# Linear attention and experts on one core: rows' turn in halves in a bank of its own, loads paced by products

## The chip, the core and the metric

One NeuronCore of a Trainium2 chip runs the whole kernel. The metric is the device time of one execution in microseconds (us); the kernel before takes 340.6 us (median of three runs, 339.92 to 341.04).

## The reference

```python
f = 1.0 / (1.0 + np.exp(-f_logit))                 # q, k, v, f_logit: [4, 8, 768, 48]
for t in range(S):
    state = f[:, :, t, :, None] * state + einsum('bhd,bhe->bhde', k[:, :, t], v[:, :, t])
    y[:, :, t] = einsum('bhd,bhde->bhe', q[:, :, t], state)
x = y as rows [3072, 384]                          # one row per token
logits = x @ w_gate; e_idx = argmax(logits)        # 8 experts, one per token
gate_w = softmax(logits)[e_idx]; eom = sigmoid(x @ w_output_gate)
out[e_idx == e] = gate_w * eom[:, e] * (relu(x @ w1[e]) @ w2[e])   # w1: [8, 384, 1024]
```

## The kernel before

**Stages.** Attention handles 24 chunks of 128 tokens (4 batches of 6, `order`), all 8 heads of a chunk at once as 4 pairs. Then the eight experts run, bound by TensorE, on rows that the attention stage has scattered into DRAM (`xs_dram`) slot by slot.

**A chunk.** With p the running product of the gates and i its inverse (scans on VectorE, L218 and L225), q becomes q\*p and k becomes k\*i (GpSimd, L232 and L229; VectorE for the first and last chunk's k). `qk` (L254) makes the 128x128 products of k and q in two row halves of the array; `mask` clears their upper triangle (VectorE for one half, ScalarE and GpSimd for the other). `kn_tr` (L273) transposes k, `state` (L290) adds k'v to the state, `state_upd` (L302 to L305) scales it, `out_state` (L317) and `out_at` (L325) make the outputs, `evac_y` (L339) copies them to `xt`, and `x_tr` (L348), the rows' turn, multiplies `xt` by a constant `turn`, which gives the token rows and, in 16 more columns per pair, the two gates' logits. `evac_x` copies both out; `route` and `slots` work out each token's expert and slot (VectorE and a few TensorE products, L431 to L436, every fourth chunk, later every second), and `scatter` (GpSimd's indirect DMA, L367) writes the rows.

**Order.** The loop at L523 emits step t; `chain` (L1230) fixes this order on every compute engine. On TensorE step t is: products of chunk t, transpose of k (not for the last chunk of a batch), rows' turn of chunk t-2, outputs of chunk t-1 from the state (not for the first chunk of a batch), outputs from the masked products, state (not for a batch's last chunk), and the rank products of `slots` where there are any. On ScalarE a step begins with one half of `evac_y`, then the gate f of chunk t+2, then the other half. Small VectorE operations of the router wait in a list and `fill` puts them between the others.

**PSUM.** Eight banks: `misc` (scratch of the state's update, the router's maxima, one chunk's f), `f_ps`, `one` (state and half of y), `two` (other half of y, ranks and counts), `kx` (two banks: transposed k in columns 0 to 255, the rows' turn in 256 to 479) and two for the products. Two accesses of one bank of one tile by different engines are put in program order, whichever columns they touch.

**Loads.** All are issued by SyncE (SP) in program order. Batches 0 and 1 are issued at the start (L479 to L485), with each chunk pair's f, k, q and v; later batches in steps 3 to 13 (L585 to L591). `clear` writes the empty rows of `xs_dram` in eight DMAs after the second batch.

**The end of attention.** Step 23 runs the rank products at its start (L553), hands over to the first expert (`hand_over`), whose first products need rows of the first 16 chunks read back from `xs_dram`.

## Time and profile before

| What | Value |
|---|---|
| Median of three runs | 340.6 us |
| The profiled execution: its time, its span | 340.03 us, 338.3 us |
| TensorE busy in the span | 327.7 us (97%) |
| Attention: first products to the last chunk's first products | 9.17 to 110.24 us |
| First expert product | 117.78 us |
| Granted TensorE clock over the span | 0.995 |

PE is TensorE's matmuls, PEld its weight loads, DVE VectorE, ACT ScalarE, POOL GpSimd, SP SyncE (SPq its DMA issues). L348 is line 348 of the kernel. A float32 product is two weight loads and two matmuls, so eight loads are four products. A weight load's start follows the engine's pace; a matmul's end is modelled.

### The profile page before, as it was taken

What the parts mean: (1) busy time and instruction counts of PE and PEld (TensorE: products, weight loads), DVE (VectorE), ACT (ScalarE), POOL (GpSimd) and SP (SyncE); (2) the same over time, 40 slices, a digit from 0 to 9 for tenths busy, and PEclk for the clock granted to TensorE, in tenths of its full rate; (3) what the DMA queues carried; (4) which work ended last, traced back from release to release, by engine and by line L of the source; (5) the groups of instructions that cost most, each with busy time, mean ns of one, the idle gap of its engine ahead of it and who ended that gap; (6) DMA issues with size and microseconds to landing.
All of it is one profiled execution on the core that took longest, in us unless ns stands there. A gap on an engine that the chain in (4) does not pass through costs nothing.

```text
span 338.3 us, 8744 instructions
## 1 busy us (share of the span) xinstructions
PE 327.7 (97%) x3119; PEld 309.2 (91%) x3119; DVE 245.0 (72%) x493; ACT 197.7 (58%) x495; POOL 196.7 (58%) x236
## 2 busy tenths in 40 slices
PE   8889999999999999999999999999999999999993
PEld 3588898898888899999999999999999999999992
DVE  5988989898989779496776767767776765764700
ACT  4477677676676574355853772773673675654510
POOL 8787789899998843010574376277276178612011
PEclk9999999999999999999999999999999999999997
DMA  7999999999713874989795395495486386521001
GB/s 247 337 348 349 310 269 260 290 291 262 227 51 124 247 298 90 258 221 245 211 255 117 122 239 149 145 225 153 124 205 190 119 213 182 200 83 41 0 25 45
DMA packets 75924, 65.68 MB, mean 194 GB/s; under 512 B 28495, under 2 KB 73332, under 8 KB 75872
## 3 DMA queue, kind: packets, MB, share of 16 engines
q1 hardware_dynamic: 71616, 55.39, 61.3%
q0 software_dynamic: 4256, 9.65, 8.5%
q8 instruction: 26, 0.43, 0.5%
q14 instruction: 26, 0.21, 0.2%
HBM read 53.73 MB, written 11.58 MB: 193 GB/s over the span
## 4 chain that ended last, share of the span: by engine, by line
PE 81%; DVE 4%; issue 4%; DMA 4%; ACT 3%; POOL 1%; SPq 1%; POOLq 0%; ACTq 0%; DVEq 0%
PE h_ps L856 30%; PE y_ps L876 21%; PE y_ps L890 9%; PE kx L348 6%; PE a_ps L254 4%; PE two_ps L325 3%; PE two_ps L317 2%; DMA v_t<-in_v 2%; PE one_ps L325 2%; PE one_ps L290 2%; DMA f_t<-in_f 2%; ACT xt L339 1%; DVE i L225 1%; DVE at L263 1%; ACT f_ps L213 1%
## 5 line engine op out<-in xcount | busy, mean ns | idle before, releaser
L911 POOL DMA_INDIRECT out<-yr,dst x67 | 74.6, 1113 | 55.3 <-ACT yr L910 33.5
L856 PE MATMUL h_ps<-xl,w1h 128*128 128x400 f32 (+5 forms) x192 | 63.7, 332 | 0.0
L856 PE MATMUL h_ps<-xh,w1h 128*128 128x400 f32 (+5 forms) x192 | 63.7, 332 | 0.0
L856 PE MATMUL h_ps<-xh,w1l 128*128 128x400 f32 (+5 forms) x192 | 63.7, 332 | 0.0
L861 DVE SCALAR_TENSOR_TENSOR hl<-h_ps,hh 128x224 fp32r<-128x224 f32 (+5 forms) x72 | 37.9, 528 | 33.6 <-ACT hh L860 33.3
L860 ACT ACTIVATE hh<-h_ps 128x224 fp32r<-128x224 f32 (+5 forms) x72 | 33.7, 469 | 40.4 <-PE h_ps L856 40.2
L876 PE MATMUL y_ps<-hh,w2h 128*128 128x224 f32 (+3 forms) x144 | 46.6, 324 | 0.0
L876 PE MATMUL y_ps<-hh,w2l 128*128 128x224 f32 (+3 forms) x144 | 46.5, 323 | 0.0
L876 PE MATMUL y_ps<-hl,w2h 128*128 128x224 f32 (+3 forms) x144 | 46.5, 323 | 0.0
L690 DVE TENSOR_TENSOR w1l<-w1r,w1h 128x768 fp32r<-128x768 f32 x31 | 29.6, 956 | 14.6 <-ACT w1h L689 14.4
L856 PEld LDWEIGHTS h_ps<-xh,w1l 128*128 128x128 f32 x192 | 36.2, 188 | 0.2
L856 PEld LDWEIGHTS h_ps<-xh,w1h 128*128 128x128 f32 x192 | 36.2, 188 | 0.2
L856 PEld LDWEIGHTS h_ps<-xl,w1h 128*128 128x128 f32 x192 | 36.2, 188 | 0.2
L232 POOL TENSOR_TENSOR q_t<-q_t,p 128x512 f32<-128x512 f32 x24 | 30.6, 1274 | 2.7 <-DVE p L218 2.3
L690 DVE TENSOR_TENSOR w2l<-w2r,w2h 128x768 fp32r<-128x768 f32 x31 | 29.7, 958 | 1.7 <-ACT w2h L689 0.9
L229 POOL TENSOR_TENSOR k_t<-k_t,i 128x512 f32<-128x512 f32 x22 | 28.2, 1281 | 3.7 <-DVE i L225 2.3
L218 DVE TENSOR_TENSOR_SCAN p<-f_ps,start_p 128x511 f32<-128x511 f32 x21 | 26.7, 1274 | 3.7 <-ACT start_p L206 2.1
L254 PE MATMUL a_ps<-q_t,k_t 64*128 64x128 f32 x384 | 27.9, 285 | 1.4 <-POOL k_t L229 1.2
L812 ACT CAST xh<-xr 128x400 fp32r<-128x400 f32 (+5 forms) x24 | 11.9, 505 | 28.7 <-DVE xr L806 25.3
L367 POOL DMA_INDIRECT xs_dram<-xn,slot x24 | 24.6, 1024 | 7.0 <-issue 3.5
L876 PEld LDWEIGHTS y_ps<-hl,w2h 128*128 128x128 f32 x144 | 27.3, 189 | 0.2
L876 PEld LDWEIGHTS y_ps<-hh,w2h 128*128 128x128 f32 x144 | 27.3, 189 | 0.2
(174 smaller groups left out, 769.1 us busy)
## 6 DMA issues: line engine op xcount, KB each, us to landing
w1r<-in_w SPq DMA_DIRECT2D x32, 384.0 KB, 4.9
w2r<-in_w SPq DMA_DIRECT2D x32, 384.0 KB, 3.7
v_t<-in_v SPq DMA_DIRECT2D x24, 256.0 KB, 7.5
f_t<-in_f SPq DMA_DIRECT2D x6, 512.0 KB, 7.8
q_t<-in_q SPq DMA_DIRECT2D x6, 512.0 KB, 9.3
k_t<-in_k SPq DMA_DIRECT2D x6, 512.0 KB
f_t<-in_f SPq DMA_DIRECT2D x12, 192.0 KB, 7.4
k_t<-in_k SPq DMA_DIRECT2D x12, 192.0 KB, 6.6
```

The source lines that it names most:

```text
L218: nc.vector.tensor_tensor_scan(out=flat(d["p"])[:, 1:n], data0=flat(d["f"])[:, 0:n - 1], data1=sp[:, 1:n], initial=sp[:, 0:1], op0=ALU.mul ...
L229: eng.tensor_tensor(out=k_t[i][:, :, sl], in0=k_t[i][:, :, sl], in1=d["i"], op=ALU.mult)
L232: nc.gpsimd.tensor_tensor(out=q_t[i][:, :, sl], in0=q_t[i][:, :, sl], in1=d["p"], op=ALU.mult)
L254: nc.tensor.matmul(aps[t][par][:, g, :], k_t[b % 2][r, g, sl], q_t[b % 2][r, g, sl], start=(g == 0), stop=(g == NP - 1))
L367: i = nc.gpsimd.indirect_dma_start(out=xs_dram, out_offset=bass.IndirectOffsetOnAxis(ap=r.slot[:, t:t + 1], axis=0), in_=xn[t // 4][:, t % ...
L690: (eng or self.nc.vector).tensor_tensor(out=to(lo), in0=of(t), in1=to(hi.bitcast(F32)), op=ALU.subtract)
L856: nc.tensor.matmul(ps[:, 0:n], a[:, c, cs], b, start=(i == 0), stop=(i == 3 * KC - 1))
L860: nc.scalar.activation(out=hi, in_=ps[:, 0:n], func=AF.Relu)
L861: nc.vector.scalar_tensor_tensor(out=lo, in0=ps[:, 0:n], scalar=0.0, in1=hi.bitcast(F32), op0=ALU.max, op1=ALU.subtract)
L876: self.nc.tensor.matmul(self.ys[d][:, c0:c0 + n], a, b, start=(f == 0 and i == 0 and part == 0), stop=(f == KF - 1 and i == 2), skip_group ...
L890: nc.tensor.matmul(ps[0:n, 0:DM], a, b[:, f % 2, :], start=(i == 0), stop=(i == 3 * KF - 1))
L911: self.other_rows(self.nc.gpsimd.indirect_dma_start(out=self.out.rearrange("n (q w) -> (n q) w", q=NQ), out_offset=bass.IndirectOffsetOnAx ...
```

## The change

The rows' turn goes to a bank of its own, `x_ps`, in two halves of 64 tokens for each pair of heads (the last two chunks in one piece). The router's ranks, counts and maxima move to the same bank's last 64 columns, the state's scratch to `two`, and in the last step both to a bank that is free then. `misc` is gone. The first half of `evac_y` is emitted right behind the outputs, ahead of `state`; `out_state` is emitted ahead of `evac_x` (TensorE's own order stays). The gates of chunks 4 and 5 are loaded ahead of v's second piece; f of chunk 4 is computed in `f_ps`. Loads from batch 1 on, and the clears, are issued one by one, each behind a product of step t, about six chunks ahead. The last chunk's inverse is written over its f in PSUM. The router's maximum and comparison are one entry of the list, and `fill` is called once more after `route`.

```diff
+LEAD = 6
-    misc = psB.tile([128, 512], F32, name="misc")
-    stmp = misc[:, 0:NP * D].rearrange("p (g e) -> p g e", e=D)
+    x_ps = psB.tile([128, 512], F32, name="x_ps")
+    kx = psA.tile([128, 2, 512], F32, name="kx")
+    def stmp():
+        return heads(spare[0][:, 64:64 + NP * D] if spare else two[:, 256:256 + NP * D], D)
+    def side_ps():
+        a = spare[0] if spare else x_ps[:, NP * XW:512]
+        return a[:, 0:40], a[:, 40:40 + E], a[:, 48:64]
+    def paced(t, half, after):
+        issued = []
+        for j in range(NCH // 2, B * NCH // 2):
+            for at, w in enumerate("fqkv"):
+                if (t, half) == divmod(2 * (2 * j - LEAD) + at, 2):
+                    b, c = divmod(2 * j, NCH)
+                    issued += load(b, [(w, c, c + 2)])
+        if half and ex.to_clear:
+            issued.append(ex.clear())
+        for i in issued:
+            tc.add_manual_dep(i.ins, after.ins.name, ... Sync, DATA ...)
-            d["f"] = {1: f_y, 2: f_o, 4: f_m}.get(ti, f_ps)
+            d["f"] = {1: f_y, 2: f_o}.get(ti, f_ps)
-            d["i"] = pf.tile([128, NP, C], F32, name="i", bufs=3)
+            d["i"] = d["f"] if ti == last else pf.tile([128, NP, C], F32, name="i", bufs=3)
 def qk(t):
+                if g == par == 0:
+                    paced(t, 0, i)
 def out_y(t):
-        y_at(t)
-        out_state(t)
-        out_at(t)
+        paced(t + 1, 1, out_at(t))
 def x_tr(t):
+        xps[t] = heads(x_ps[:, 0:NP * XW], XW)
+        step = 64 if t < last - 1 else C
         for g in range(NP):
-            nc.tensor.matmul(xps[t][:, g // 2, g % 2, :], xt[t][:, g, :], turn[:, g, :], ...
+            for j in range(0, C, step):
+                nc.tensor.matmul(xps[t][j:j + step, g, :], xt[t][:, g, j:j + step], turn[:, g, :], ...
+        def best():
+            one = side_ps()[2][:, 0:n].unsqueeze(2)
+            red(out=one, in_=lg, axis=AX.X, op=ALU.max)
+            tt(out=r.ohb[:, gi, 1:n + 1, :], in0=lg, in1=one.broadcast_to([128, n, E]), op=ALU.is_equal)
-    load(0, [("v", 2, 4), ("fkqv", 4, 6)])
-    load(1, [("fkqv", 0, 2), ("fkqv", 2, 4), ("fkqv", 4, 6)])
+    load(0, [("f", 4, 6), ("v", 2, 4), ("kqv", 4, 6)])
-    load(2, [("f", 0, 2)])
-    ex.clear()
         if hot(t - 2):
-            evac_y(t - 2, (0,))
             state_upd(t - 2)
...
         evac_kn(t)
+        if hot(t - 1):
+            y_at(t - 1)
+            out_state(t - 1)
         pre(t + 2, "mul_q", *(("ends",) if t != 1 else ()))
...
         if hot(t - 1):
             out_y(t - 1)
+            if t < last:
+                evac_y(t - 1, (0,))
         if hot(t - 1):
             state(t - 1)
...
-        if t >= 3 and b + 2 < B and c in (0, 2, 4):
-            ...
         if t - 2 in ends:
             route(*ends[t - 2])
+            fill(more)
```

## Rows read from the trace of the kernel before

**Rows 1.** The page: the chain's shares by engine, and loads of f (us to landing)
```profile
PE 81%; DVE 4%; issue 4%; DMA 4%; ACT 3%; POOL 1%; SPq 1%; POOLq 0%; ACTq 0%; DVEq 0%
...
f_t<-in_f SPq DMA_DIRECT2D x6, 512.0 KB, 7.8
```
**Rows 2.** Stretches, steps 4 and 12 to 19: us; busy PE, PEld, DVE, ACT, POOL; clock, DMA
```profile
26.32:30.82 4.50, 4.50 (x85) 4.09 (x82) 3.91 (x7) 3.19 (x10) 3.18 (x4) 1.00 1.09 346
61.83:96.37 34.54, 34.20 (x584) 30.77 (x580) 30.98 (x55) 25.42 (x80) 32.36 (x35) 1.00 0.93 246
```
**Rows 3.** The weight loads of step 4 in order of time (start us, us)
```profile
26.32 0.97 PEld L254 LDWEIGHTS a_ps<-q_t,k_t 64*128 64x128 f32 x16
27.21 0.38 PEld L273 LDWEIGHTS kx<-ident,k_t 64*128 64x128 f32 x8
27.66 0.97 PEld L348 LDWEIGHTS kx<-turn,xt 128*128 128x128 f32 x8
28.74 0.14 PEld L317 LDWEIGHTS two_ps<-q_t,state 64*64 64x64 f32 x2
...
29.34 0.20 PEld L325 LDWEIGHTS two_ps<-at,v_t 128*64 128x64 f32 x4 [0.17 <-issue]
...
30.16 0.60 PEld L290 LDWEIGHTS one_ps<-v_t,kn 128*64 128x64 f32 x16
30.81 0.97 PEld L254 LDWEIGHTS a_ps<-q_t,k_t 64*128 64x128 f32 x16
```
**Rows 4.** Weight loads in order of time: the rows' turn of steps 5 and 7
```profile
32.16 0.52 PEld L348 LDWEIGHTS kx<-turn,xt 128*128 128x128 f32 x4 [0.37 <-ACT xt L339]
...
40.23 0.38 PEld L273 LDWEIGHTS kx<-ident,k_t 64*128 64x128 f32 x8
40.90 0.97 PEld L348 LDWEIGHTS kx<-turn,xt 128*128 128x128 f32 x8 [0.29 <-ACT xt L339]
41.98 0.20 PEld L325 LDWEIGHTS two_ps<-at,v_t 128*64 128x64 f32 x4
```
**Rows 5.** In order of time: loads, gate and first rows' turn before 19 us
```profile
9.95 1.10 SPq L186 DMA_DIRECT2D v_t<-in_v  x2
11.19 0.38 SPq L191 DMA_DIRECT2D f_t<-in_f  x1
17.02 1.22 DVE L225 TENSOR_TENSOR_SCAN i<-f_ps,start_i 128x512 f32<-128x512 f32 x1
17.30 0.38 PEld L273 LDWEIGHTS kx<-ident,k_t 64*128 64x128 f32 x8
17.60 0.21 ACT L206 ACTIVATE start_p<-f_t 128x4 f32<-128x4 f32 x1 [1.97 <-DMA f_t<-in_f]
18.69 0.97 PEld L348 LDWEIGHTS kx<-turn,xt 128*128 128x128 f32 x8 [1.00 <-ACT xt L339]
```
**Rows 6.** GpSimd in order of time: scatters, k's products, masks of late steps
```profile
62.70 1.01 POOL L367 DMA_INDIRECT xs_dram<-xn,slot  x1 [0.79 <-DVE misc L304]
94.08 1.29 POOL L229 TENSOR_TENSOR k_t<-k_t,i 128x512 f32<-128x512 f32 x1
97.68 1.01 POOL L367 DMA_INDIRECT xs_dram<-xn,slot  x1 [0.50 <-DVE top L419]
111.93 0.65 POOL L260 TENSOR_SCALAR_AFFINE_SELECT at<-at 128x512 f32<-128x512 f32 x1
```
**Rows 7.** In order of time: ranks on VectorE, and rows' turns behind them
```profile
62.01 0.19 DVE L439 TENSOR_TENSOR rk<-two_ps,ohb 128x32 f32<-128x32 f32 x1 [0.48 <-PE two_ps L433]
63.16 0.97 PEld L348 LDWEIGHTS kx<-turn,xt 128*128 128x128 f32 x8
111.40 0.97 PEld L348 LDWEIGHTS kx<-turn,xt 128*128 128x128 f32 x8
112.26 0.16 DVE L439 TENSOR_TENSOR rk<-two_ps,ohb 128x16 f32<-128x16 f32 x1
113.07 0.20 PEld L325 LDWEIGHTS two_ps<-at,v_t 128*64 128x64 f32 x4 [0.17 <-issue]
```

## The prediction

> **What bounds the kernel now.** The chain of waits comes first: TensorE holds 81% of it [rows 1]. So the question is what the change does to TensorE's time until the first expert product; behind that, products follow each other to the end, and what attention gains the whole execution gains. Next, the busy times by stretch [rows 2]: step 4 lasts 4.50 us with TensorE busy for all of it; from step 12 to step 19 (34.54 us) TensorE is busy 34.20, but GpSimd already 32.36, and the rest of GpSimd's time is mostly the 0.17 us ahead of each scatter. Third, the weight loads of one step [rows 3]: products at 26.32, transpose at 27.21, rows' turn at 27.66, outputs from the state at 28.74, from the products at 29.34, state at 30.16, next step at 30.81. No load waits for another engine; the idle 0.17 at 29.34 is put down to nothing and appears where the shape of the product changes. An ordinary step is thus the sum of its products, 4.49 us.

> **The rows' turn in halves.** Now eight loads, four products of 128 by 128, take 27.66 to 28.74, which is 1.08 us, of which some 0.17 is the change of shape, so 0.91 [rows 3]. Afterwards there are sixteen loads of 128 by 64. The nearest row is the outputs from the products, with the same shape, four groups of four loads, 128 columns against 112: 29.34 to 30.16, 0.82 us. If columns bound it, the halves take 0.82 x 112/128 = 0.72; if the loads do, 0.82. The saving is 0.09 to 0.19 per chunk. I take 0.12, because the whole products run at 0.91/8 = 0.11 per load where 112 columns would allow 0.82/8 x 112/128 = 0.09, so loads count. Bound below nothing: halves that don't overlap in pairs would cost 16 x 0.11 = 1.8, that is 0.9 more per chunk.

> [...]

> Where no outputs from the state follow (steps 7, 13, 19), the halves are followed by products of their own shape, so the 0.17 goes too. In step 7 the turn also starts 0.67 after the transpose (40.23 to 40.90, idle until ScalarE's copy) against 0.45 in step 4 [rows 3, 4]: 0.22 more. Step 7 gives 0.39 beside the 0.12.

> **The first half of the outputs' copy sooner.** In steps without a transpose (5, 11, 17) the turn waits for the second copy: 30.81 to 32.16 is 1.35, though the products take 0.89 and the change of shape 0.17 [rows 3, 4]. With one copy ahead of the state the copies end some 0.8 us sooner, so 0.28 goes each time. What is late next there is nothing on TensorE. ScalarE's queue behind the moved copy holds the second half, then f and the mask's copy; the second half waits for the state's products as before, so none starts later. In ordinary steps this hides behind the products and is worth nothing.

> **The gates of chunk 4 sooner.** ScalarE stands 1.97 us until 17.60 for that load, and the first turn waits 1.00 behind it, starting at 18.69 [rows 5]. The load moves ahead of two issues of v that took 9.95 to 11.19, so 1.24 us sooner; v lands as much later, needed only in step 3, past 24 us. The turn is then held by its own transpose, 17.30 + 0.45 + the 0.17 that the row order leaves, say 17.92: it gains 0.77, not 1.24. f of chunk 4 in `f_ps` must wait for the scan that ends at 17.02 + 1.22 = 18.24; it would otherwise start about 17.4, was at 18.52, so VectorE gains only about 0.3 there, and its slack per step (4.50 against 3.91 busy) [rows 2] makes that up within two steps. If the load gains nothing, the term is 0.

> **Loads behind products, clears one by one.** Cost taken as nothing. SP waits, and behind the waiting issue stand only later loads. A pair's f is issued at the start of step 2j-6 and first read at the end of step 2j-3, over three steps of 4.4 us later; landing takes 7.8 us [rows 1]. The cover is some 6 us; if it went, ScalarE's queue would stand as at 17.60. A gain from quieter DMA I bound by 0, since no load is waited for after 18 us.

> **The bank of its own, the scratch in `two`, fill, the last inverse.** `kx` no longer ties the transpose's copy to the turn: ScalarE gets up to 1 us of slack per step that nothing on TensorE waits for, so 0. The scratch in `two` follows a copy that ends sooner and precedes outputs that wait for the state anyway: 0. But ranks and turn now share a bank. In step 12 the ranks are read at 62.01 to 62.20 and the turn starts at 63.16, 0.96 later [rows 7]: free. In step 23 the rank products come ahead of the turn: it starts at 111.40, the ranks are read until 112.42 [rows 7]. The turn must wait: about 1.08 us of new stall. Emitting outputs from the state sooner leaves TensorE's order as it is, and the router's entries move by one place on VectorE, inside its slack: 0. The last inverse in PSUM changes one VectorE product off the path: 0, at most 0.3 either way.

> **The sum.** Until step 12: 0.77 + ten turns x 0.12 = 1.20 + steps 5 and 11, 0.56 + step 7, 0.39 = 2.92. From there GpSimd sets the pace. Its scatter at 62.70 had waited 0.79 for the ranks [rows 6], so it moves with TensorE; but up to 97.68 there are eight scatters in 34.98 us with one idle 0.50, 4.31 per step, without a pause beyond issue. k's product for chunk 20 ends at 94.08 + 1.29 = 95.37, TensorE's step 20 begins at 96.37 [rows 2, 6]: TensorE may gain another 0.9 until it waits for k (its own sum, seven turns with step 17's 0.28 and steps 13 and 19, would be 1.7). GpSimd itself gains the 0.33 that the pause at 97.68 is over an issue: 3.25. TensorE comes to step 23 with 2.92 + 0.92 and two or three turns more, about 4.1, and loses 1.08 to the ranks: 3.0. GpSimd's mask, 0.49 ahead of its reader (112.58 against 113.07) [rows 6, 7], allows 3.25 + 0.49, so it doesn't bind. The profiled execution's 340.03 becomes 337.0; it lies 0.57 under the median, so the median becomes 337.6.

> **Rivals.**
> 1. *GpSimd doesn't hold it and the ranks don't either* (they are read before the turn is due): TensorE's own sum, 2.92 + 1.7 + 0.3 = 4.9, less up to 0.5 for the mask; 336.2. For it: GpSimd's idle 0.50. Against: 4.31 per step repeated eight times. Chance 0.12.
> 2. *Halves save nothing*: the 0.91 stays; 0.77 + 0.56 + 0.39 = 1.72 until step 12, then under GpSimd's pace some 0.6 more, less about 0.8 for the ranks: 1.5; 339.1. For it: loads already count in the whole products. Chance 0.14.
> 3. *Slower: VectorE holds the shared bank.* Place: `x_ps` in the steps behind ranks (8, 12, 16, 20, 22, 23). Each time VectorE reads the ranks later than 0.96 us after now, the turn stands and everything behind it. It decides from a mean delay of 0.8 past that margin: five more stalls of 1.0 with the forecast's one make 3.0 - 5.0 = 2.0 slower, 342.6. For it: in steps 9 to 12 VectorE has 3.91 of 4.4 us, and the router's operations come on top. Against: it still waited 0.48 for the rank products at 62.01 [rows 7]. Chance 0.05.
> 4. *Slower: halves add to the whole's time instead of overlapping.* The state's sixteen loads with only 48 columns take 30.16 to 30.81, 0.65 us, 0.04 each [rows 3]; eight more loads at that price beside 0.91 are 0.32 per chunk, 7.0 over 22 chunks, against 1.7 of the other terms: 345.9. It decides above 0.08 per chunk. Against: the 0.82 of the same shape. Chance 0.03. [...]
> 5. *The first term fails* (the gates still land at 17.6, or q behind them is late): 3.0 less 0.8; 338.4. Chance 0.11.

> The forecast, 337.6, has 0.55; its own range is 336.9 to 338.3. To 0.8 the range takes in cases 1, 2 and 5 with the bounds of the turn (22 x 0.03 below to 0.07 above): 335.9 to 340.0. A measurement here tells 0.3%, 1.0 us, from no change. Faster by more than that: 0.55 + 0.12 + 0.11 and a little of case 2, 0.80. Within it: most of the rest of case 2, 0.10. Slower: cases 3 and 4 with 0.02 for what no row shows, 0.10.

> **What would show it.** The turn: sixteen loads of 128 by 64 from its first load to the next operation's in about 0.94 (0.77 in steps 7, 13, 19). The first turn near 17.9 with no idle time put down to ScalarE. Steps of 4.37 from 4 to 11, the first products of step 12 near 58.9. Then scatters 4.31 apart without pause and TensorE's idle time put down to k's product. In step 23 a turn that starts behind the ranks, 1 us after its rank products. First expert product near 114.8. Wrong it would be if the halves took over 0.9, if VectorE's ranks came later than the turn in step 12, or if ScalarE waited for loads after 20 us.

## The result and the profile after

The changed kernel takes 345.54 us (median of five runs, 342.45 to 345.68) against 340.6: a ratio of 1.013, 95% interval 1.0108 to 1.0153. It is slower by 1.3%, where 0.9% faster was forecast. A second timing on another chip gave 1.0131 (1.0074 to 1.0189). The profiled execution took 345.54, with a span of 343.8. Ratios and their intervals leave out runs that lie over 1.5% above the fastest of the same kernel.

First the page of the changed kernel: shares of the chain of waits, and the queue that brings instructions (packets, MB, share of 16 engines; 26 packets and 0.43 MB before).

```profile
PE 75%; DMA 6%; issue 6%; DVE 5%; POOL 2%; SPq 2%; ACT 2%; POOLq 0%; ACTq 0%; DVEq 0%
...
q8 instruction: 28, 0.46, 0.6%
```

TensorE holds less of the chain than before [rows 1], and "issue", time for which no wait is shown, holds more. Where that lies on TensorE is told by its waits from 20 us to the start of step 22 (us in total, times, longest).

```profile
PEld two_ps L354 <- issue: 2.8, 16, 0.2
PEld a_ps L281 <- POOL k_t L256: 1.2, 2, 0.8
PEld two_ps L346 <- issue: 1.2, 1, 1.2
PEld x_ps L375 <- issue: 1.0, 3, 0.4
PEld x_ps L375 <- ACT f_ps L240: 0.6, 1, 0.6
PEld one_ps L318 <- issue: 0.6, 1, 0.6
PEld kx L301 <- issue: 0.5, 1, 0.5
PEld a_ps L281 <- issue: 0.5, 2, 0.3
PEld one_ps L354 <- issue: 0.4, 1, 0.4
PEld L463 <- issue: 0.4, 1, 0.4
```

The 2.8 us in 16 pieces is the 0.17 at a change of shape [rows 3]; the same view of the kernel before has 2.6 of it, and 0.3 ahead of its products beside. Of the seven other "issue" rows here, the one of L281 stands ahead of products as well, and the one of L463 is a wait after all: a weight load can show no releaser where its matmul names one. The matmuls' waits of the same stretch have two on the shared bank.

```profile
PE x_ps L375 <- DVE ohb L435: 0.5, 1, 0.5
PE x_ps L461 <- ACT xn L384: 0.4, 1, 0.4
```

The first is the turn of step 21, held until VectorE's comparison has read its maximum (in the weight loads' view above it is put down to ScalarE's f, 0.6); the second is the ranks of step 19, held until ScalarE has copied the rows. The remaining five rows are new. They hold six breaks of 0.35 to 1.21 us, 3.4 us together, each in the middle of a group of equal products. Step 4 in order of time shows one.

```profile
25.61 0.97 PEld L281 LDWEIGHTS a_ps<-q_t,k_t 64*128 64x128 f32 x16
26.50 0.38 PEld L301 LDWEIGHTS kx<-ident,k_t 64*128 64x128 f32 x8
26.95 0.77 PEld L375 LDWEIGHTS x_ps<-turn,xt 128*64 128x64 f32 x16
27.87 0.14 PEld L346 LDWEIGHTS two_ps<-q_t,state 64*64 64x64 f32 x2
...
28.63 0.25 PEld L354 LDWEIGHTS one_ps<-at,v_t 128*64 128x64 f32 x3
29.24 0.13 PEld L354 LDWEIGHTS one_ps<-at,v_t 128*64 128x64 f32 x1 [0.35 <-issue]
...
30.43 0.19 PEld L281 LDWEIGHTS a_ps<-q_t,k_t 64*128 64x128 f32 x2
```

The turn itself does what was forecast: 26.95 to 27.87, 0.92 against 1.08. But at 28.63 four loads on the same bank break after the third, wait for nothing, and go on at 29.24. The step lasts 4.82 instead of 4.50.

Second, the end of attention: stretches of step 22, of step 23 up to the turn, of what follows, and up to the first expert product (us; busy PE, PEld, DVE, ACT, POOL; granted clock, DMA share, GB/s).

```profile
106.41:110.81 4.40, 4.39 (x91) 3.89 (x88) 3.60 (x11) 2.52 (x7) 3.88 (x4) 1.00 0.34 115
110.81:114.10 3.29, 1.33 (x23) 1.11 (x19) 2.59 (x6) 1.47 (x3) 2.95 (x4) 0.95 0.92 270
114.10:119.80 5.70, 5.67 (x69) 4.98 (x69) 0.98 (x5) 0.97 (x3) 1.97 (x2) 0.50 0.91 281
119.80:122.86 3.06, 3.06 (x43) 2.61 (x41) 2.80 (x10) 1.84 (x6) 1.49 (x2) 0.87 1.05 399
```

TensorE is busy for 1.33 of 3.29 us, and then the granted clock is 0.50 for 5.7 us. From the start of step 23 to the first expert product it is 12.05 us; it was 7.54 (110.24 to 117.78). What TensorE stood for, in order of time:

```profile
110.11 0.18 DVE L426 TENSOR_REDUCE ohb<-ohb 128x8 bf16<-128x24 bf16 x1
110.31 0.37 ACT L367 COPY xt<-two_ps 128x256 f32<-128x256 f32 x1 [0.91 <-DVE ohb L426]
110.58 0.83 ACT L713 CAST w1h<-w1r 128x768 fp32r<-128x768 f32 x1
111.44 1.20 DVE L714 TENSOR_TENSOR w1l<-w1r,w1h 128x768 fp32r<-128x768 f32 x1 [1.16 <-ACT w1h L713]
111.92 0.12 PEld L463 LDWEIGHTS <-ones 128*128 128x128 bf16 x2
113.22 0.68 DVE L292 TENSOR_TENSOR at<-a_ps,mask 128x512 f32<-128x512 f32 x1
113.82 0.17 DVE L469 TENSOR_TENSOR rk<-x_ps,ohb 128x16 f32<-128x16 f32 x1
114.10 1.44 PEld L375 LDWEIGHTS x_ps<-turn,xt 128*64 128x64 f32 x16 [2.06 <-issue]
114.13 1.76 PE L375 MATMUL x_ps<-turn,xt 128*64 128x112 f32 x16 [2.00 <-DVE rk L469]
```

Read upwards: the turn starts when the ranks have been read (113.82), as its matmul's row names; VectorE is late there since its w1l began only at 111.44; it waited 1.16 for ScalarE's w1h, which stood behind the copy of xt's first half. That copy is the one that the change moves ahead. In the kernel before VectorE read the ranks 2.02 after the step's start (112.26 [rows 7] less 110.24), now 3.01. That the moved copy makes the cast late is read from this order; no run put the copy back.

What the clock costs differs between executions. In a second trace of the changed kernel (a0_after below) the stall is 2.06 again, but the clock is 0.58 from 114 to 118 us and 1.00 behind that, and step 23 takes 10.70 up to the first expert product instead of 12.05. The run of 342.45 shows a granted clock of 0.997 over its span, the other four 0.986 to 0.990.

### The profile page after: what moved, and what is told of

Read it like the earlier page. It is cut to its first block, busy times and chain, and to the rows that moved or that the text cites. A ratio compares the mean times of both kernels' runs of the same rounds, so it can differ in the third digit from the quotient of the medians.

```text
span 343.8 us, 9110 instructions
## 1 busy us (share of the span) xinstructions
PE 327.2 (95%) x3295; PEld 308.2 (90%) x3295; DVE 244.8 (71%) x492; ACT 197.4 (57%) x495; POOL 195.8 (57%) x236
## 4 chain that ended last, share of the span: by engine, by line
PE 75%; DMA 6%; issue 6%; DVE 5%; POOL 2%; SPq 2%; ACT 2%; POOLq 0%; ACTq 0%; DVEq 0%
PE h_ps L880 30%; PE y_ps L900 20%; PE y_ps L914 8%; PE a_ps L281 4%; PE x_ps L375 4%; PE two_ps L354 2%; DMA v_t<-in_v 2%; PE two_ps L346 2%; DMA w2r<-in_w 2%; PE one_ps L354 2%; PE one_ps L318 2%; DVE p L245 2%; DVE i L252 1%; DMA f_t<-in_f 1%; DVE at L292 1%
## 5 line engine op out<-in xcount | busy, mean ns | idle before, releaser
L935 POOL DMA_INDIRECT out<-yr,dst x67 | 73.5, 1096 | 54.8 <-ACT yr L934 33.6
L245 DVE TENSOR_TENSOR_SCAN p<-f_ps,start_p 128x511 f32<-128x511 f32 x22 | 28.0, 1275 | 5.0 <-ACT f_ps L240 2.7
L281 PE MATMUL a_ps<-q_t,k_t 64*128 64x128 f32 x384 | 28.0, 284 | 3.7 <-POOL k_t L256 2.0
L281 PEld LDWEIGHTS a_ps<-q_t,k_t 64*128 64x128 f32 x384 | 23.5, 187 | 6.3 <-POOL k_t L256 3.0
L375 PE MATMUL x_ps<-turn,xt 128*64 128x112 f32 (+1 forms) x368 | 25.0, 272 | 2.8 <-DVE rk L469 2.0
```

The source lines that it names most:

```text
L245: nc.vector.tensor_tensor_scan(out=flat(d["p"])[:, 1:n], data0=flat(d["f"])[:, 0:n - 1], data1=sp[:, 1:n], initial=sp[:, 0:1], op0=ALU.mul ...
L281: i = nc.tensor.matmul(aps[t][par][:, g, :], k_t[b % 2][r, g, sl], q_t[b % 2][r, g, sl], start=(g == 0), stop=(g == NP - 1))
L375: nc.tensor.matmul(xps[t][j:j + step, g, :], xt[t][:, g, j:j + step], turn[:, g, :], start=(g == 0), stop=(g == NP - 1), skip_group_check= ...
L935: self.other_rows(self.nc.gpsimd.indirect_dma_start(out=self.out.rearrange("n (q w) -> (n q) w", q=NQ), out_offset=bass.IndirectOffsetOnAx ...
```

## The experiments

Two losses were to be priced: the stretches without a wait (theory A: the halves' instructions; theory B: the loads behind products) and step 23 (my theory: the ranks' wait, and the clock with it; the rival: VectorE's other work). The kernel before took 339.8 to 341.6 on three chips; on four others (most runs below) it took 362 to 381 itself, all kernels losing their time behind step 22, so from these only the traces to that point are read, and of step 23 whether TensorE stood and at what clock, not how long it lasted. On those chips every variant stood above the kernel before, by 1.5 to 3.3% in medians, also the one that loses nothing on a chip of the first kind; why was not settled. A packet border is one of the places in TensorE's stream, about 130 weight loads apart, on which the breaks fall; the section on why the prediction was wrong sets them beside the packets of instructions.

**The kernels as they are.** 

> The kernel before, unaltered, for its trace on the chips of these runs, where it takes about 374. To step 22 its trace should be that of the 340.6 us run within 0.3 (step 16 at 79.0, step 22 at 105.7), since the changed kernels' traces agree to there as well; what it loses should lie behind step 22 and in the experts' part.

> The changed kernel, unaltered, on the same chips. If the loss behind step 22 is the same for all kernels: 374 and the 5 us of the first comparison, 379. If it falls harder on kernels that reach the experts' part with TensorE waiting: as the experiments, 383 to 385. Idle stretches at the borders of instruction packets at the same products as in its first trace (28.7, 35.6, 49.2 us).

Both met a chip of the first kind: 340.17 and 344.40. The kernel before began steps 3 to 23 some 0.4 sooner than in its first trace (step 22 at 105.35), which is the grain of what follows. The changed kernel had six such breaks again, 3.0 us together, two of them at other products than in its first trace.

**The turn in one piece.**

```
-        step = 64 if t < last - 1 else C
+        step = C
```

> The turn in one piece (8 loads of 128 columns, not 16 of 64), all else as in the changed kernel. Theory A (the idle stretches inside groups of products, about 4 us from 22 to 78 us, each 1 to 1.7 us after a packet of instructions, come of the halves' extra 352 TensorE instructions): they go, as in the kernel before; the halves' own gain of 0.12 per chunk (2.6 in all) is lost; about 344. Theory B (they come of loads that are now issued behind products, whose packets run while the instructions are fetched): they stay; about 348. By both, the stall at the ranks in step 23 and the fall of the granted clock behind it stay.

Then twice more, 

> The same kernel as e1_whole (turn in one piece, the rest as changed), timed again: in e1_whole the kernel before itself took 362 to 377, and of its trace only the stretch to step 22 could be set beside the others. There its step 22 began at 104.47 against 106.41 in the changed kernel and 105.75 in the kernel before. Theory A (halves raise the rate of instructions over what is fetched): where the kernel before takes about 340.5, it takes 2 less than the changed kernel, 343.5, with no idle stretch inside a group of products between 22 and 100 us, and the stall and the low clock of step 23 unchanged. Theory B: 347 or more.

> Turn in one piece, all else as changed; beside a kernel before at about 340.8. Theory A: no idle stretch at packet borders between 22 and 100 us, step 22 begins at 104.5 as in e1_whole, 2 us before the changed kernel's; the ranks' stall and the low clock stay: 342.5 to 343.5. Theory B: 347.

Step 22 began at 104.47, 105.07 and 104.83; the times, 382.88, 385.29 and 383.79, are those of the slower chips. TensorE's waits of the first run from 20 us to there, of those for nothing shown, are the usual ones alone:

```profile
PEld two_ps L354 <- issue: 2.6, 15, 0.2
...
PEld a_ps L281 <- issue: 0.5, 3, 0.2
```

Theory A holds: the six breaks have become none, and step 22 comes 1.3 to 1.9 sooner than in the changed kernel though each turn takes longer. The low clock of step 23 stayed (0.68 from 114 to 118 us).

**The loads as before.** `paced` returns at once; the loads and clears stand where they were. 

> Loads and clears issued as in the kernel before (batches 0 and 1 at the start, the fifth chunk's gates still ahead; the others in steps 3, 5, 7), nothing waits for a product; halves, bank, ranks as in the changed kernel. Theory B (paced loads disturb the fetch of instructions): the stretches of about 4 us go, about 341.5. Theory A (the halves' instructions): they stay, about 345.5. By both the stall at the ranks and the fall of the clock stay.

And again, 

> Loads and clears issued as in the kernel before, all else as changed (halves and ranks as changed). Theory A: the stretches at packet borders stay, in part at other borders since other transfers run beside the fetches; 344 to 346. Theory B: 341.5.

The stretches stayed: five breaks of the same kind, 3.3 us, up to step 22, which began at 106.19 (110.32 in a repetition, e2c_loads, with 5.0 us of them). From the same view, rows that the kernel before has not:

```profile
PEld two_ps L347 <- DVE p L246: 1.3, 1, 1.3
PEld x_ps L376 <- issue: 1.0, 3, 0.4
...
PEld L464 <- issue: 0.7, 1, 0.7
PEld one_ps L319 <- issue: 0.5, 1, 0.5
PEld kx L302 <- issue: 0.5, 1, 0.5
...
PEld one_ps L355 <- issue: 0.4, 1, 0.4
```

The first row is put down to VectorE, but lies at a border of packets like the others (90.52). One of the three of x_ps is the shared bank, which the matmul's row names (70.87, 0.28 for VectorE's comparison). L319's is at the end of step 21 (105.46); from there to step 23 the slower chips show more breaks, with whole turns too. Theory B falls.

**Halves alone, in the kernel before.**

```
         for g in range(NP):
-            nc.tensor.matmul(xps[t][:, g // 2, g % 2, :], xt[t][:, g, :], ...
+            for j in range(0, C, 64):
+                nc.tensor.matmul(xps[t][j:j + 64, g // 2, g % 2, :], xt[t][:, g, j:j + 64], ...
```

> The kernel before with one part of the change alone: the turn in 64-token halves, in the two banks that it had. Theory A: the halves save 0.1 per chunk where TensorE is the bound, but TensorE then takes some 130 pairs of weight load and product in under 7 us here and there, and idle stretches of 0.3 to 1 us appear at borders of instruction packets, fewer than in the changed kernel since the wait for xt still slows its steps; step 22 begins at 105.0 to 106.5. Theory B: no such stretches, step 22 at 104 (20 chunks at 0.1 sooner).

On a chip where the kernel before took 340.82, ten runs spread from 340.75 to 350.12, median 344.57; the ratio is 1.0042 (1.0012 to 1.0072). What the stretches cost thus differs much between executions. The profiled run, 344.93, began step 22 at 108.88, 3.5 later than the kernel before on this chip. Its waits to there:

```profile
PEld two_ps L325 <- issue: 2.6, 15, 0.2
...
PEld kx L350 <- issue: 1.6, 2, 1.1
PEld one_ps L290 <- issue: 1.3, 1, 1.3
PEld one_ps L317 <- issue: 1.2, 1, 1.2
PEld L435 <- issue: 1.0, 1, 1.0
...
```

So one part by itself makes the stretches, more of them than I expected: seven breaks, 5.8 us. Its step 23, in which ranks and turn have banks of their own, took 7.48 up to the first expert product at the full clock, while the changed kernel on the same chip took 10.70. The mechanism is theory A's; my size for it, step 22 at 105.0 to 106.5, was too small.

**Ranks of step 23 elsewhere.**

```
-        a = spare[0] if spare else x_ps[:, NP * XW:512]
+        a = spare[0] if spare else kx[:, 1, NP * XW:512] if late else x_ps[:, NP * XW:512]
```

with `late` filled at the last step, where `kx` is free. 

> In step 23 alone the ranks are written to a free part of the banks of k's transposes, not to the bank of the turn. My theory: the idle stretch of about 2.0 us between the ranks' products and the turn goes, and with it the fall of the granted clock to 0.50 from 114 to 120 us (2.5 to 3 us); together 4 to 4.5 less, about 341.3. Rival: the clock falls anyway, since TensorE is thinly busy in steps 22 and 23 whatever the ranks do: about 344.5. Second rival: TensorE waits for VectorE's other work behind it and the idle stretch only moves to the products after the turn: about 345.

Repeated twice: 

> The same kernel as e3_ranks (only the ranks of step 23 elsewhere), timed again. Its trace kept the full clock from 110 to 126 us, where the changed kernel ran at 0.50 to 0.68. My theory: 4 less than the changed kernel, about 341.5, with the idle stretches at the borders of instruction packets as they were. Rival (the time only moves to VectorE's other work before the turns of step 23): 344.

> Only the ranks of step 23 elsewhere. My theory: the 2.0 us stall and the 2.5 to 3 us of the low clock go, 340.5 to 341.5; the stretches at packet borders stay. Rival (VectorE's other work holds the turns of step 23 all the same, the clock falls or the time is lost to waits): 344.

In step 23 of the first run (114.84 to the first expert product at 124.01) the turn followed the ranks' products at once, at 116.09, and the clock stayed full, though TensorE was busy for only 4.58 of the last 6.01 us:

```profile
114.00:118.00 4.00, 3.44 (x67) 2.87 (x67) 2.29 (x6) 2.57 (x6) 1.16 (x3) 1.00 0.94 258
118.00:124.01 6.01, 4.58 (x79) 3.87 (x76) 3.62 (x16) 1.98 (x7) 3.12 (x4) 1.00 1.03 361
```

The clock stayed full in step 23 of both repetitions too. The breaks at packet borders stayed (4.4, 2.8 and 3.2 us in the three traces). One of them, 2.3 us up to 78.50 in the first run, was followed by a granted clock of 0.50 (80.00 to 81.81) far from step 23: a low clock behind a stall there as well. All three runs met slower chips, so this repair was never timed alone where the kernel before takes 340. With the loads as before too, 

> The loads as before and the ranks of step 23 elsewhere, both. Theory B with my theory of the ranks: 341.5 less 4.2, about 337.4, which is what the forecast's sum came to. Theory A with it: as the ranks alone, about 341.3. If the clock falls anyway: about 340.5 with B.

it was the same: clock 1.00 from 106 to 126 us, the longest breaks 2.2, 1.0 and 0.8 us. The prices could not be read there.

**Both repairs.** 

> Turn in one piece, ranks of step 23 elsewhere, loads behind products as changed. Theory A and my theory of the ranks: both repairs add up, 345.5 less 2 less 4, about 339.5, a little under the kernel before. If they don't add (the low clock of step 23 comes of something that both share): 341.5.

> The kernel of e5_whole_ranks again, to be timed where the kernel before takes about 340.5, since in all runs so far both it and the others lost 30 to 40 us behind step 22. Theory A and my theory of the ranks: 339.5, 1 under the kernel before. If the low clock comes back by another wait of step 23: 342.

> Turn in one piece and ranks elsewhere, loads behind products. If the two repairs add: 338.5 to 339.5, faster than the kernel before by 0.4 to 0.7%. If the time regained to step 22 is lost to the same waits of step 23: 341.

These three met slower chips (383.67, 379.16, 382.98; step 22 at 104.63, 105.18, 105.03); the fourth met one where the kernel before took 340.34. 

> Turn in one piece and ranks of step 23 elsewhere, the rest as changed; in its traces so far step 22 began at 104.6 to 105.2 (kernel before: 105.4 to 105.8) and the clock stayed at 1.00 until the ranks' place was passed. Where the kernel before takes 340.6: if the ranks' stall and the clock were the rest of the loss, 339 to 340. If the kernel loses 5 us at step 23 for another reason, as the wait for xt seen at 117.5 us in its traces would have it: 342.

It took 339.99 (339.61 to 341.29): 0.9993 of the kernel before, 0.9981 to 1.0004. The whole 1.3% is back, and no more. Up to step 22 this is the kernel of e1_whole, now on a chip of the first kind: no break, and step 22 at 104.58, 1.7 to 1.8 sooner than in the two traces of the changed kernel (106.41, 106.27). From step 22 on, stretches as above for the changed kernel (step 22, step 23 up to the outputs from the state, and up to the first expert product):

```profile
104.58:109.06 4.48, 4.48 (x83) 4.08 (x80) 3.47 (x11) 2.52 (x7) 3.91 (x5) 1.00 0.35 111
109.06:111.54 2.48, 2.31 (x32) 2.01 (x28) 1.81 (x4) 1.61 (x5) 2.47 (x4) 1.00 0.81 215
111.54:116.51 4.97, 4.97 (x92) 4.27 (x92) 4.25 (x17) 2.44 (x9) 3.40 (x5) 1.00 0.92 272
```

No thin stretch, no low clock, and 7.45 from step 23 to the first expert product at 116.51.

**The loads as before, beside both repairs.** 

> As e5_whole_ranks, and the loads issued as in the kernel before. If the loads behind products are worth nothing: as e5, about 339.5. If they are what brings steps 9 to 22 of e1_whole forward by 1.3 against the kernel before: 340.8. If they disturb (theory B): 337.

> Turn in one piece, ranks of step 23 elsewhere, loads and clears issued as in the kernel before. If loads behind products cost nothing, as forecast: 340.0, as e5d_whole_ranks. If their packets slow the steps from 40 us on (e6_whole_ranks_loads began steps 11 to 22 by 0.2 to 0.4 sooner than e5_whole_ranks): 339.5, 0.25% under the kernel before, the fastest of all. If they help: 340.5 or more.

Both runs met slower chips only: 382.18 and 382.36, level with e5_whole_ranks (383.67) for those spreads. Step 22 began at 104.19 and 104.57, against 104.58 to 105.18 in the four traces with the loads behind products. What these are worth is thus open, within about half a us up to step 22.

## Why the prediction was wrong

**The failed step: the turn in halves.** The forecast priced it by the time of its loads, and that was right: 0.92 in step 4, and in step 7 40.32 to 41.05, 0.73 (forecast 0.94 and 0.77). What eight more loads and products per chunk ask of the supply of instructions it put at nothing, without a reason. Instead of the 2.4 that twenty turns at 0.12 would have given, the changed kernel begins step 22 1.83 later than the same kernel with whole turns (106.41 against 104.58): a swing of 4.2 us. The six breaks are 3.4 us of idle time, and each costs some 0.1 more than that (an estimate from step 4: 4.82, where e5d_whole_ranks has 4.48 and the halves save 0.12, so 0.46 for an idle 0.35).

How the supply fails is read from the traces; no run changed the supply itself. Packets of queue 8, of 16384 bytes each, start through the whole execution, at 26.52, 33.73, 40.36, 46.90 and 54.01 in the changed kernel; there are 28 in every kernel with halves and 26 in every one without. Counted in weight loads and the few control records of its stream, the breaks fall on number 230, 359, 488, 747, 877 and 1266: 129 or 130 apart, or twice or three times that. In every run with halves, on every chip, the breaks inside a group of equal products fall on such borders up to step 20 (617, 1007, 1396 and 1527 too; the numbers are a few higher in the halved kernel before). In the changed kernel TensorE goes on 2.4 to 2.9 us after such a packet starts (at 29.24 for that of 26.52). Between 20 and 80 us, where the DMA share is 1.10 (20 to 60 us) and 1.09 (60 to 84), the packets start 3.2 to 4.8 us after TensorE passed the border before. Together that is up to 7 us and more for one packet. Where nothing stalls, TensorE with halves runs from border to border in 6.3 to 6.6 us (36.18 to 42.80, 56.66 to 62.92). With whole turns 129 loads take about 7.1 us, an estimate from step 4 (82 in 4.50 [rows 2]); up to 80 us the packets of the kernel before start 6.7 to 8.4 us apart, and it does not break. That queue 8 feeds TensorE is the author's reading of these counts; how far ahead of TensorE packets come, and what one waits for before it starts, no run shows.

**The mis-sized step: ranks ahead of the turn.** The ranks' place in the turn's bank was foreseen, at 1.08; TensorE stood 2.06. The forecast took VectorE's time of before. But the copy of xt's first half, moved ahead, stands before the weight's cast on ScalarE, and VectorE's subtraction, mask and ranks wait behind that cast, 1 us later than before. The text named what is queued behind the moved copy as the second half, f and the mask's copy, and left out the cast of step 22. The low clock behind the stall was not thought of at all: stall and clock together turn 7.45 into 12.05, 4.60 us more (3.25 in the second trace), and both went when the ranks moved. Of the 8.1 us between the first expert product as forecast (114.8) and as measured (122.86), 4.2 belong to the halves and 3.5 to this step.

**What held.** The first turn began at 17.72 (17.92 forecast) and step 3 at 20.94 (0.9 sooner, 0.5 against the second trace). Step 5's turn stands 1.09 behind the step's start (30.43 to 31.52) against 1.35: 0.26 for 0.28. No load was waited for on ScalarE after 20 us. Without halves the forecast has 1.72 gained at step 12 (its rival 2); e5d_whole_ranks has 1.58 (1.17 against the second trace). GpSimd then sets the pace, as said, but earlier: TensorE waits for k's product in steps 13 and 14,

```profile
65.60 0.52 PEld L281 LDWEIGHTS a_ps<-q_t,k_t 64*128 64x128 f32 x8 [0.46 <-POOL k_t L256]
...
69.91 0.41 PEld L281 LDWEIGHTS a_ps<-q_t,k_t 64*128 64x128 f32 x5 [0.79 <-POOL k_t L256]
```

(the changed kernel; 0.6 in all in e5d_whole_ranks), and of the 0.9 that was to come after step 12 nothing was kept: step 20 of e5d_whole_ranks begins 1.68 sooner than before (94.69 against 96.37), but in step 21 its turn waits 0.51 for VectorE's comparison in the shared bank, as in the changed kernel. The forecast looked at the ranks in that bank and not at the maxima. So 1.27 is gained at the first expert product without halves and stall (0.87 against the second trace), and the medians show 0.35 of it. The last expert product begins 1.29 sooner (331.00 against 332.29), but 7.2 us follow from there in that trace and 6.0 in the first of before; what sets these last scatters was not tried.

**The rivals.** Rival 4 gave 345.9, and 345.5 was measured, yet it is wrong: the halves do overlap (the whole turn took 0.92 in step 4, not the 1.40 of 1.08 and 0.32). A time that fits is no proof; the row of the turn is, sixteen loads in 0.77 us. Rival 3 had VectorE holding the shared bank in six steps by its ranks; it did so in step 23, and by its maximum in step 21, and ScalarE held it in step 19. Of the three signs that the forecast named against itself, none told: the turn took 0.75 beside its change of shape, the ranks of step 12 were read ahead of the turn, and ScalarE waited for no load after 20 us. The whole loss is 5.08 at the first expert product: 1.27 gained, 1.75 lost to halves (1.83 at step 22 less 0.08 in that step), 4.60 lost in step 23.

## What to carry to other kernels

When a change cuts one instruction into several, count what TensorE executes per packet of instructions and compare the time with that from one packet to the next in the trace; a stretch that waits for nothing, inside a group of equal products, at equal counts in every run, is the sign (here about 130 loads, in 6.3 to 6.6 us with halves where nothing stalls, and up to 7 us and more for a packet). Look at the matmul's row beside its weight load's before you call a stretch a wait for nothing. Before a bank is shared, list everything that reads it, and follow each reader's queue back through both engines with the moved instructions in it. And read the granted clock of the stretch that follows a stall: here a stall of 2.06 us came with a clock of 0.50 or 0.58 behind it, and the two cost 3.25 to 4.60.
